# Transposing loads in the head, row-group score matmuls and a fifth Toeplitz buffer in a gated attention and state-space kernel

## The chip, the core and the metric

The kernel runs on one core of a Trainium2 chip, in bf16 with float32 sums. The metric is the device time of one execution in microseconds (us). TensorE does matmuls and their weight loads, ScalarE activations, VectorE and GpSimd elementwise work; SP, ScalarE and GpSimd issue DMAs, which 16 DMA engines carry out.

## The reference

Two branches of 2048 tokens and 448 channels are mixed by a gate for each token:

```
g = sigmoid(sum(x * gate_w))                       # one number a token
q = x @ wq  (16 heads of 28);  k = x @ wk;  v = x @ wv      # one K and V for all heads
a = softmax(q k^T / sqrt(28)) v @ wo               # all 2048 x 2048 scores, for 16 heads
K[d,l] = Re sum_n C[d,n] exp(dt[d] A[d,n] l) dt[d] B[d,n]   # n = 256, l = 0..2047
y = causal convolution of x with K along the tokens + Dskip * x
out = g * a + (1 - g) * y
```

A, B and C are complex, given as real and imaginary parts of shape 448 x 256; dt is exp(log_dt). The input of the convolution is x as well; B_u is not used.

## The kernel before, in words

**Attention.** Q, K and V are projected from x transposed (channels on partitions). The Q rows are laid out in groups of 32 partitions, one head each (28 rows and one row for a bound that is subtracted ahead of the exponential). There are 1024 score tiles of 128 keys x 512 queries: 16 steps (4 groups of heads x 4 quarters of the queries) of 64 tiles. They are put into sets of alternately three and two tiles, 410 in all. For each set TensorE computes the scores into five PSUM banks (`qk`, L1117), ScalarE takes one exponential over the whole set into a ring of 15 tiles (L1153), and TensorE multiplies four tiles with V (`pv`, L1157 and L1163). A score matmul is made in one of two ways: by row groups (L1125), where the matmuls of a set take 29 rows each in different row groups of the array, or at full height (L1133), with a copy of Q in which the rows of all other heads are zero (`qM`). The first six sets and, from the fourteenth on, the sets of three use row groups; the others use full height. `qM` is filled for every step by four small DMAs from GpSimd's queue, in `qproj` (L764).

**Convolution.** `prep_params` (L686) makes seeds from A, B, C and dt; `masters` and `tables` on VectorE build powers of the exponentials for 32 channels at a time; `kgen` (L898) multiplies them into K on TensorE; K goes through a DRAM scratch, and `tload` (L946) brings it back as Toeplitz matrices of 128 x 1024 for four channels at a time (T buffers, four of them, and later three in the space that the used-up U leaves). `conv` (L959) multiplies them with U, which holds x by token blocks.

**Head.** x is loaded in four quarters, transposed on TensorE against an identity (L597), copied from PSUM by ScalarE (L607) and VectorE (L609), and projected. The largest absolute key (`kap`, L640) gives the bound row `Wb` that the second part of the Q projection (L783) needs, so the first scores wait for all of K. The six parameter arrays are loaded and transposed in the same way (L713). U is made from staged rows of x with copies on GpSimd (L550) and a DMA of U onto U.

**The order of the work.** Each engine runs a fixed list, written by a planner in the program (`schedule`, L158) from assumed durations and priorities: lower priority numbers go first among what can start at the same time. Its constants include `SLACK`, by which work of priority 2 and more is put off. Every edit to an operation or an assumed duration can therefore change the order on every engine. DMAs of one queue start in that order; each T, K and U load is issued by SP, the K stores and small attention DMAs by GpSimd.

The functions that the change touches, and what calls them, with the line numbers of the profile:

Of the kernel before, what the change touches and what calls it, by code (L numbers as in the profile page):

```python
# [19 lines left out]
DT = 112  # L20
# [11 lines left out]
NTR = 4  # L32
# [3 lines left out]
XQ = NT * 512  # L36
SIN2PI = 6.2831850
# [37 lines left out]
class Prog:  # L75
# [11 lines left out]
    SLACK = {"pe": 500.0, "dve": 1000.0}  # L87
# [45 lines left out]
    def dma(self, pairs, desc, slot, rd=(), wr=(), pr=0, eng="sp", slow=False, extra=0):  # L133
        kw = dict(allow_slow_non_contiguous=True) if slow else {}

        def fn(e):
            return [e.dma_start(o, i, **kw) for o, i in pairs]  # L137
        nd, size = desc
        ns = 10.0 if size < 64 else 13.0 + 0.033 * size if size < 1500 else 8.0 + 0.0372 * size
        o = self.op(eng, fn, nd * ns / 16.0 * (1.15 if size < 1500 else 1.8 if nd < 512 else 1.0), rd, wr, pr)  # L140
# [233 lines left out]
def el(n, rate=0.96, fix=68):  # L374
    return fix + n / rate
# [15 lines left out]
class Kernel:  # L391
# [25 lines left out]
    def alloc(self):  # L417
# [7 lines left out]
        self.qM = sb("qM", 2 * 4 * 512, BF)  # L425
# [35 lines left out]
        self.XS = nc.dram_tensor("XS_scratch", (3 * DT * XQ,), BF).ap()  # L461
        self.R = nc.dram_tensor("R_scratch", (16 * 4 * 512,), F32).ap()

    def consts(self):
# [5 lines left out]
        dm(V(self.cst, 512, 256), 0.0, 170, [("cst", 1)])  # L470
        pm(V(self.ident, 0, P), 1.0, 200, ["id"])
# [13 lines left out]
        for k in range(2):  # L485
            pm(V(self.qM, k * XQ, XQ), 0.0, 1800, [("qM", k)], 1.5)
        pm(V(self.identf, 0, P), 1.0, 200, ["msq"], 2)
        pg.op("pool", lambda e: e.affine_select(
            out=V(self.identf, 0, P), in_=V(self.identf, 0, P), compare_op=ALU.is_equal, fill=0.0,
            base=0, pattern=[[-1, P]], channel_multiplier=1), 300, rd=["msq"], wr=["msq"], pr=2)  # L490
        self.sel = self.onT.cast(F32)
# [8 lines left out]
    def loads(self):  # L500
        pg, ins = self.pg, self.ins
        self.xst = self.tab
        x = ins["A_x"]

        def lx(q):
            pg.dma([(self.xst.v(0, P, q * 4 * D, [[1, 4 * D]]), dram(x, q * 4 * P * D, [[4 * D, P], [1, 4 * D]]))],
                   (128, 3584), f"x{q}", wr=[("xst", q)])
# [5 lines left out]
        def lraw(k):  # L513
            pg.dma([(raw.v(0, DT, k * 1024, [[1, 1024]]), dram(ins[names[k]], 0, [[1024, DT], [1, 1024]]))],
                   (112, 2048), f"raw{k}", wr=[("raw", k)])
# [4 lines left out]
        pg.dma([(wks.v(0, DT, 0, [[1, 112]]), dram(ins["A_wk"], 0, [[112, DT], [1, 112]])),  # L520
                (wks.v(0, DT, 112, [[1, 112]]), dram(ins["A_wv"], 0, [[112, DT], [1, 112]])),
# [62 lines left out]

    def prep_x(self):
        pg = self.pg
        xst, kT = self.xst, self.kT
        sm = self.small
        for q in range(4):
            for hp in range(2):  # L590
# [657 lines left out]
```

## Time and profile before

| | us |
|---|---|
| median of 3 runs | 521.37 (519.04 to 526.63) |
| the profiled execution | 521.35 |
| its span | 519.4 |
| ScalarE busy | 483.6 (93%) |
| VectorE busy | 447.5 (86%) |
| TensorE busy | 431.1 (83%) |
| GpSimd busy | 161.6 (31%) |
| first exponential starts | 27.69 |
| last exponential ends | 504.17 |
| mean granted TensorE clock | 0.95 |

A group of instructions is shown as line, engine, operation, tiles, shape and count, then the busy time, the mean duration of one in ns, and the idle time just before them with what ended it. The mean durations of overlapping instructions add up to more than the busy time: an exponential over three tiles takes 1561 ns and one over two 1139, but one starts before the other is done, and 410 of them keep ScalarE busy for 465.8 us. The granted clock is 1.00 at full speed.

### The profile page before, as it was taken

The numbers are of one execution on the slowest core, as the hardware profiler recorded it, in microseconds if no ns is written. First come the engines' busy times: TensorE is split into PE (matmuls) and PEld (weight loads), VectorE is DVE, ScalarE is ACT, GpSimd is POOL, SyncE is SP. The second block draws the span as 40 slices with busy tenths as digits, with TensorE's granted clock in tenths as the row PEclk, the third lists the DMA queues.
The fourth block names the chain that finished last, engine by engine and source line by source line (L and its number), as shares of the span: only waits on it lengthen the run. The fifth ranks groups of instructions, "written<-read, shape, count | busy, mean of one in ns | idle before, by whom it ended". The sixth has DMA issues, their size and how long they took to land.

```text
span 519.4 us, 18307 instructions
## 1 busy us (share of the span) xinstructions
PE 431.1 (83%) x8123; PEld 192.9 (37%) x8234; DVE 447.5 (86%) x798; ACT 483.6 (93%) x431; POOL 161.6 (31%) x299
## 2 busy tenths in 40 slices
PE   5778967888878789988878889988888889798884
PEld 4522111324334334434333434433344344443342
DVE  3877899999999999999999979999999989952123
ACT  3699899999999999999999999999999999899980
POOL 5014321612413442424214242432414233315100
PEclk9858587979999999999999999999999999999998
DMA  8995395497991998899998899899996999999996
GB/s 263 259 236 157 28 79 139 120 364 251 288 365 54 321 350 256 271 342 347 316 367 296 279 373 276 285 336 350 329 330 212 304 370 353 346 282 305 376 365 172
DMA packets 121997, 144.31 MB, mean 278 GB/s; under 512 B 53860, under 2 KB 60564, under 8 KB 121920
## 3 DMA queue, kind: packets, MB, share of 16 engines
q1 hardware_dynamic: 112368, 133.06, 81.3%
q0 software_dynamic: 8896, 9.53, 6.8%
q8 instruction: 64, 1.05, 0.8%
q10 hardware_dynamic: 656, 0.57, 0.4%
q14 instruction: 13, 0.11, 0.1%
HBM read 128.76 MB, written 5.23 MB: 258 GB/s over the span
## 4 chain that ended last, share of the span: by engine, by line
ACT 40%; DVE 36%; PE 17%; DMA 3%; issue 2%; ACTq 0%; SPq 0%
ACT expT L1153 40%; DVE tab L868 6%; PE psS L1133 4%; DVE tab L880 3%; DVE tab L879 3%; DVE tab L878 3%; PE psB L1163 3%; PE psS L1125 3%; DVE tab L890 3%; DVE tab L877 3%; DMA T<-KP_scratch 2%; DVE tmp L886 2%; DVE msq L811 1%; DVE cst L984 1%; PE psX L915 1%
## 5 line engine op out<-in xcount | busy, mean ns | idle before, releaser
L1153 ACT ACTIVATE expT<-psS 128x1536 bf16<-128x1536 f32 (+1 forms) x410 | 465.8, 1349 | 8.1 <-PE psS L1125 5.3
L1133 PE MATMUL psS<-qM,kT 128*128 128x512 bf16 x308 | 106.6, 402 | 35.5 <-ACT expT L1153 21.7
L1125 PE MATMUL psS<-qT,kT 29*128 29x512 bf16 x609 | 84.0, 401 | 27.8 <-ACT expT L1153 23.4
L1163 PE MATMUL psB<-expT,vaug 128*32 128x512 bf16 x1024 | 105.4, 403 | 1.1 <-ACT expT L1153 0.6
L137 POOL DMA_DIRECT2D KP_scratch<-kstg x112 | 62.3, 563 | 121.3 <-DVE kstg L930 114.6
L868 DVE TENSOR_TENSOR tab<-tab,mbf 128x512 bf16<-128x512 bf16 (+3 forms) x56 | 64.5, 1152 | 0.0
L1163 PEld LDWEIGHTS psB<-expT,vaug 128*32 128x32 bf16 x1024 | 26.2, 93 | 83.2 <-issue 78.7
L137 POOL DMA_DIRECT2D qM<-qT x64 | 32.0, 507 | 67.9 <-DVE qT L786 42.9
L1125 PEld LDWEIGHTS psS<-qT,kT 29*128 29x128 bf16 x609 | 20.1, 91 | 72.6 <-ACT expT L1153 60.2
L1133 PEld LDWEIGHTS psS<-qM,kT 128*128 128x128 bf16 x415 | 26.0, 98 | 54.8 <-ACT expT L1153 40.2
L137 POOL DMA_DIRECT2D rdenB<-R_scratch x60 | 30.5, 514 | 38.5 <-DMA R_scratch<-denT 27.9
L880 DVE TENSOR_TENSOR tab<-tab 128x128 bf16<-128x128 bf16 (+4 forms) x70 | 41.8, 597 | 0.0
L879 DVE TENSOR_TENSOR tab<-tab 128x128 bf16<-128x128 bf16 (+4 forms) x70 | 41.8, 597 | 0.0
L974 PE MATMUL psS<-T,U 128*32 128x128 bf16 (+7 forms) x1600 | 39.0, 220 | 2.2 <-DMA T<-KP_scratch 1.3
L974 PEld LDWEIGHTS psS<-T,U 128*32 128x32 bf16 (+7 forms) x1600 | 27.1, 94 | 18.1 <-issue 12.2
L137 POOL DMA_DIRECT2D denT<-acc x15 | 10.9, 726 | 69.1 <-DVE acc L1030 45.0
L890 DVE TENSOR_TENSOR tab<-tab,tmp 128x4096 bf16<-128x4096 bf16 x14 | 32.1, 2290 | 0.1
L878 DVE TENSOR_TENSOR tab<-tab,mbf 128x4096 bf16<-128x4096 bf16 x14 | 31.9, 2280 | 0.1
L877 DVE TENSOR_TENSOR tab<-tab,mbf 128x4096 bf16<-128x4096 bf16 x14 | 32.0, 2283 | 0.0
L974 PE MATMUL psX<-T,U 128*32 128x128 bf16 (+7 forms) x1216 | 29.9, 223 | 1.0 <-issue 0.9
L974 PEld LDWEIGHTS psX<-T,U 128*32 128x32 bf16 (+7 forms) x1216 | 21.0, 95 | 14.7 <-issue 11.3
L915 PE MATMUL psX<-tab 128*32 128x64 bf16 x1024 | 24.8, 241 | 1.1 <-DVE qT L786 0.4
(153 smaller groups left out, 517.1 us busy)
## 6 DMA issues: line engine op xcount, KB each, us to landing
T<-KP_scratch SPq DMA_DIRECT2D x176, 512.0 KB, 8.7
U<-KP_scratch SPq DMA_DIRECT2D x48, 512.0 KB, 9.6
rdenB<-R_scratch POOLq DMA_DIRECT2D x60, 64.0 KB, 5.7
U<-cst SPq DMA_DIRECT2D x1, 3584.0 KB, 18.7
qM<-qT POOLq DMA_DIRECT2D x64, 32.0 KB, 5.1
tab<-in_A_x_dram SPq DMA_DIRECT2D x4, 448.0 KB, 6.2
O<-in_A_x_dram SPq DMA_DIRECT2D x16, 112.0 KB, 2.7
O<-cst SPq DMA_DIRECT2D x1, 1792.0 KB, 28.6
```

Source lines behind the costliest of these rows:

```text
L137: return [e.dma_start(o, i, **kw) for o, i in pairs]
L868: vo(lambda e, dst=dst, src=src, mri=mri: e.tensor_tensor(dst, src, mri, ALU.mult), 4 * n, done + mk(lv), [kr, ki, tk])
L877: vo(lambda e, src=src, mi=mi, tv=tv: e.tensor_tensor(tv, src, mi, ALU.mult), 2 * n, done + mk(lv), [tk])
L878: vo(lambda e, dst=dst, src=src, mr=mr: e.tensor_tensor(dst, src, mr, ALU.mult), 2 * n, done + mk(lv), [kr, ki, ("gap", s)])
L879: vo(lambda e, dc=dc, tc=tc: e.tensor_tensor(dc[0], dc[0], tc[1], ALU.subtract), n, [tk, kr], [kr])
L880: vo(lambda e, dc=dc, tc=tc: e.tensor_tensor(dc[1], dc[1], tc[0], ALU.add), n, [tk, ki], [ki])
L890: vo(lambda e: e.tensor_tensor(tab.v(0, P, FM, [[4, 1024], [1, 4]]), tab.v(0, P, lo + 124, [[CG, 32], [-4, 32], [1, 4]]), rho.v(0, P, 0, [ ...
L974: r = e.matmul(ps.v(32 * j, 32 - 2 * n, 128 * k, [[1, 128]]), self.U.v(0, P, (4 * gi + j) * 32 + 2 * n, [[1, 32 - 2 * n]]), tbuf.v(0, P, t ...
L1125: r = e.matmul(self.psS.v(0, P, 512 * b, [[1, 512]]), kT.v(32 * h, DH + 1, 128 * kt, [[1, 128]]), qT.v(32 * h, DH + 1, 512 * (i % 2), [[1, ...
L1133: return e.matmul(self.psS.v(0, P, 512 * b, [[1, 512]]), kT.v(0, P, 128 * kt, [[1, 128]]), self.qM.v(0, P, (i % 2) * XQ + 512 * h, [[1, 51 ...
L1153: pg.op("act", lambda e: e.activation(expT.v(0, P, 512 * es[0], spread(es, n)), self.psS.v(0, P, 512 * bs[0], spread(bs, n)), AF.Exp, scal ...
L1163: r = e.matmul(self.psB.v(32 * h, 32, 0, [[1, 512]]), vaug.v(0, P, 32 * kt, [[1, 32]]), expT.v(0, P, 512 * ring[t], [[1, 512]]), start=(kt ...
```

## The change

- x is loaded by transposing DMAs straight into its transposed place, in quarters of 512 tokens, with channels in three blocks of 128 and one of 64 instead of four of 112 (`KT`). The last 16 tokens of the last block come by a small DMA of single elements. The transposes on TensorE and the copies from PSUM are gone, and the weights of the projections are loaded in the same blocks.
- The six parameter arrays are loaded by transposing DMAs; the products on VectorE read SBUF instead of PSUM. Products of priority 3 are placed behind the maximum of the keys.
- U is loaded straight from x, in rows of 256 B (128 B in the last region); its layout is now region, token block, channel, so the stationary operand of the convolution has a step of 128 channels between its columns. The staging, GpSimd's copies and the DMA of U onto U are gone.
- All score sets use row groups; `qM`, its memsets and its DMAs are gone.
- There are five T buffers from the start (`NTR`).
- `kgen` writes both halves of K into one PSUM bank and stores them with one addition and one copy instead of two each; the four T loads of a convolution stand together ahead of its matmuls.
- The planner's `SLACK` for VectorE goes from 1000 to 700 ns, and a float32 identity for the gate moves into another buffer.

```diff
-NTR = 4
+NTR = 5
+KT = (128, 128, 128, 64)
-    SLACK = {"pe": 500.0, "dve": 1000.0}
+    SLACK = {"pe": 500.0, "dve": 700.0}
...
+            if flip:
+                return [e.dma_start_transpose(o, i) for o, i in pairs]
...
-        self.qM = sb("qM", 2 * 4 * 512, BF)
...
         def lx(q):
-            pg.dma([(self.xst.v(0, P, q * 4 * D, [[1, 4 * D]]), dram(x, q * 4 * P * D, [[4 * D, P], [1, 4 * D]]))],
-                   (128, 3584), f"x{q}", wr=[("xst", q)])
+            xT, xo = self.xq(q)
+            at = lambda off, n, m: xT.v(0, P, xo + off, [[512, n], [1, m]])
+            r = q * 512 * D
+            if q < 3:
+                pg.dma([(at(0, 4, 512), dram(x, r, [[D, 512], [1, 512]]))], (512, 1024), f"x{q}", wr=self.xk(q), flip=True, cost=1900)
+                return
+            pg.dma([(at(0, 3, 512), dram(x, r, [[D, 512], [1, 384]])),
+                    (at(1536, 1, 496), dram(x, r + 384, [[D, 496], [1, 128]]))],
+                   (512, 896), f"x{q}", wr=[("xT", q)], flip=True, cost=1900)
...
         def lraw(k):
-            pg.dma([(raw.v(0, DT, k * 1024, [[1, 1024]]), dram(ins[names[k]], 0, [[1024, DT], [1, 1024]]))],
-                   (112, 2048), f"raw{k}", wr=[("raw", k)])
+            pg.dma([(raw.v(0, P, k * 1024, [[D, 2], [1, D]]), dram(ins[names[k]], 0, [[NM, D], [1, NM]]))],
+                   (448, 512), f"raw{k}", wr=[("raw", k)], flip=True, cost=900)
...
+        xT, xo = self.xq(3)
+        pg.dma([(xT.v(0, 64, xo + 2032, [[1, 16]]), dram(x, 2032 * D + 384, [[1, 64], [D, 16]]))],
+               (1024, 2), "x4", wr=[("xT", 4)], eng="act", slow=True)
...
+        part = lambda r, odd, off, dims: bass.AP(tensor=self.U.h, offset=odd * rs + r * TW + off, ap=[[2 * rs, 64]] + dims)
+        for r in range(4):
+            w = min(128, D - 128 * r)
+            self.late.append(pg.dma(
+                [(part(r, 0, 16 * w, [[256, w // 16], [1, 256]]), self.cst.v(0, 64, 512, [[0, w // 16], [1, 256]])),
+                 (part(r, 0, 0, [[w, 16], [1, w]]), dram(x, 128 * r + 960 * D, [[D, 64], [-64 * D, 16], [1, w]])),
+                 (part(r, 1, 0, [[w, 32], [1, w]]), dram(x, 128 * r + 1984 * D, [[D, 64], [-64 * D, 32], [1, w]]))],
+                (3584, 2 * w), f"u{r}", rd=[("cst", 1)], wr=[("U", r)], pr=0.3).i)
...
         def trans(k, pr):
-            t_ = self.grp()
...
-            pg.op("pe", mm, 700, rd=[("raw", k), "id"], wr=[X, "rawdone"], pr=pr, lock=t_)
-            return t_, X
+            return raw.v(0, P, k * 1024, [[D, 2], [1, D]]), ("raw", k)
...
-            pg.dma([(self.qM.v(32 * h, 32, s * XQ + 512 * h, [[1, 512]]), self.qT.v(32 * h, 32, 512 * s, [[1, 512]]))
-                    for h in range(4)], (128, 1024), f"qm{s}", rd=[("q", s)], wr=[("qM", s)], pr=0, eng="pool", extra=4500)
...
+        pg.op("dve", lambda e: e.tensor_copy(ko.v(0, P, 0, [[64, 8], [1, 63]]), G.v(0, P, 0, [[64, 8], [1, 63]])),
+              el(504), rd=[X], wr=["kst"], pr=2, unlock=G)
...
-                                     self.U.v(0, P, (4 * gi + j) * 32 + 2 * n, [[1, 32 - 2 * n]]),
+                                     self.U.v(0, P, uo + 2 * n * uw + j, [[uw, 32 - 2 * n]]),
...
-            if s < 6 or s >= 14 and len(ts) == 3:
-                rd = set()
...
-            else:
-                for t, b in zip(ts, bs):
...
+            pg.op("pe", row, 220, rd=sorted(rd, key=str), wr=bk, pr=0, mode="q", ni=2 * len(ts))
```

## The prediction

> **What bounds the kernel now.** I read the page from the top, then busy time by stage, the stretches in which the clock was low, the waits, and the timeline at both ends of ScalarE's work. The columns of a stretch are: window, its length, busy us and instructions of TensorE, weight loads, VectorE, ScalarE and GpSimd, then the granted clock, the DMA engines' share and GB/s.
>
> ```profile
> PE 431.1 (83%) x8123; PEld 192.9 (37%) x8234; DVE 447.5 (86%) x798; ACT 483.6 (93%) x431; POOL 161.6 (31%) x299
> ...
> L1153 ACT ACTIVATE expT<-psS 128x1536 bf16<-128x1536 f32 (+1 forms) x410 | 465.8, 1349 | 8.1 <-PE psS L1125 5.3
> L1133 PE MATMUL psS<-qM,kT 128*128 128x512 bf16 x308 | 106.6, 402 | 35.5 <-ACT expT L1153 21.7
> L1125 PE MATMUL psS<-qT,kT 29*128 29x512 bf16 x609 | 84.0, 401 | 27.8 <-ACT expT L1153 23.4
> ```
>
> ScalarE is busy for 93%, and 465.8 us of that are the 410 exponentials, which wait only 8.1 us in all. Most waits of the score matmuls are for the exponential.
>
> ```profile
> 27.69:504.17 476.48, 406.39 (x7791) 174.62 (x7900) 424.01 (x752) 468.80 (x414) 153.96 (x277) 0.95 0.90 281
> ...
> 460.00:480.00 20.00, 17.29 (x451) 8.65 (x457) 7.36 (x12) 20.00 (x19) 9.45 (x18) 1.00 0.94 297
> ```
>
> The first exponential starts at 27.69; the last ends at 504.17. Between them ScalarE is busy 468.80 of 476.48 us, so 7.7 us is lost there. The chain that ended last gives VectorE 36%, but from 460 VectorE is busy 7.36 of 20 us while ScalarE still has 44 us to go: two saturated engines run side by side, and ScalarE is the one that ends late. The span is thus 27.7 (before the first exponential) + 476.5 + 15.2 (after the last) = 519.4; the profiled execution took 521.35, so 1.95 lies around the span, and the median of the runs (521.37) is the same. Three terms can move: the head, the 7.7 us of holes, the tail. The exponentials themselves don't change.
>
> ```profile
> 50.59:64.25 13.66, 12.94 (x53) 2.40 (x55) 11.77 (x28) 11.76 (x11) 6.13 (x6) 0.50 0.33 24
> 84.73:91.55 6.82, 5.92 (x81) 1.80 (x81) 6.82 (x15) 6.53 (x6) 0.00 (x0) 0.50 0.09 16
> 105.21:112.03 6.82, 6.15 (x59) 1.67 (x56) 6.82 (x9) 5.89 (x6) 0.56 (x1) 0.50 1.06 395
> ...
> 120.00:440.00 320.00, 278.57 (x5866) 126.68 (x5937) 312.35 (x558) 318.20 (x282) 108.53 (x200) 1.00 0.93 305
> ```
>
> Of the 7.7 us, 1.90 + 0.29 + 0.93 = 3.1 are in these three stretches at a clock of 0.50, 0.9 more before 42 us, also cold, and 1.8 in the 320 us from 120 on, where the clock was 1.00 (the rest, some 1.9, is at 92 and around 450). So a cold TensorE costs ScalarE about 1 us per stretch of 7 to 14 us, and a warm one almost nothing.
>
> **The change, part by part.**
>
> *Head.* Today x goes through 64 transposes on TensorE (7.4 us busy), four copies of 1.02 us on ScalarE and four of 1.21 on VectorE; two of the parameters go through TensorE too before the first exponential. All of that is removed, and the DMA engines transpose. The new chain: the last x quarter lands, its keys are projected, ScalarE copies them, VectorE takes their maximum, and the second half of the Q projection follows. In the changed order VectorE is given the product with A_re ahead of the last maximum and the product with B_re ahead of the last Q copy, so both must have landed as well. On the SP queue they stand behind all of x: three quarters of 512x512 and one of 520 KB are 2.09 MB, and the three parameters up to B_re 0.69 MB; ScalarE's queue adds W_q and log_dt, 0.52 MB. No transposing DMA is in the trace. Its nearest rows by size are these: copies in pieces of 448 B moved at 30 ns a piece on each of 16 engines, which is 237 GB/s. The end below is a plain load: the 3,584 B pieces of x were all started by 10.5 us, though seven loads shared the engines. The end above is the copy U<-U in pieces of 32 B: 0.92 MB between 58.35 and 76.56 us, 50 GB/s.
>
> At 237 GB/s, 3.30 MB take 13.9 us; with the issue at 0.81 and some 2.5 until data flow (the first load had landed at 4.29), the last x quarter is there at about 15, A_re at 16.2, B_re at 17.2. TensorE has had little to do by then, so I take the cold row for its key projection (1.89; warm it took 1.03): 15.2 + 1.9 = 17.1, key copy 0.69, maximum 0.68 (18.5), the last maximum and Wb 0.4 (18.9, with its semaphore 19.0), then in order on VectorE the B_re product 1.08, the V copy 0.58 and the Q copy 0.69 (21.4), then the scores, 0.63. First exponential at **22.0** instead of 27.69: **-5.7**. With a plain load's landing the same chain gives 17 to 18 (-10), with the 32 B rate 2.78 MB last 56 us and the first exponential comes at some 63 (+35); I take the middle row because its pieces are nearest in size to the rows that are transposed. The head breaks even when B_re lands 5.7 us later, at 23, which is about 165 GB/s.
>
> [...]
>
> *Score matmuls.* 410 weight loads and as many matmuls with the zero-padded Q (full height) become row-group matmuls of 29 rows, which run beside each other: a set of two cost 0.60 us full and 0.39 by row groups when warm, 1.03 and 0.60 when cold. 205 sets x 0.21 = 43 us less work for TensorE. None of it lies on the path while ScalarE is busy, so I count it at nothing; it is worth something only in the holes. The 64 Q copies on GpSimd's queue (0.50 us each, 32 us) and two 1.8 us memsets go as well; GpSimd is busy 31%, its other DMAs mostly wait for VectorE, and nothing ended later because of it.
>
> *The clock* is what that could cost. From 36.9 to 40.4 us every set used the padded form, and at 40.35 the clock rose to 1.00; in the mixed stretches it fell again at 50.59, 71.07, 84.73 and 105.21 whenever no table or convolution matmuls ran, and from 112 on, where they did, it stayed at 1.00 for 402 us. With fewer cells at work I expect TensorE cold through the first phase, until the convolutions come (the changed order has them 40 score tiles, some 18 us, earlier), and a few cold stretches later. When cold, row groups need 1.03 - 0.60 = 0.4 us less a pair, which takes the holes of 38.55 and 41.15 away (0.9); the first Q projection into a cold array stays (1.9), the first convolution too (0.9). I take three more cold stretches than before at about 0.9 us each: -0.9 + 2.7 = **+1.8**.
>
> *Fifth buffer and smaller things.* One hole, 0.80 us at 266, was a wait for a Toeplitz buffer's load, which five buffers should hide; the last convolution's pieces, now out of the end, cost 0.68 + 0.42 = 1.1 there, since the changed order has no convolution left after the last exponential: **-1.9**. Storing K as one eviction instead of two saves VectorE about 28 x 0.41 - 14 x 0.68 = 2.0 us and 2.4 of the small additions; VectorE isn't what ends, so nothing. The first half of K now waits for the second (64 matmuls, at 40 in 0.81 some 1.3 us) before GpSimd stores it, beside a landing of 8.7 us for the load behind it. On SP the eleven transposing issues, at 0.43 as plain ones, are hidden by their own data; x reloads and the scratch copies of x become two issues each, off the path. U is loaded in rows of 256 B instead of through staging, eight GpSimd copies of 1.03 and a 20 us copy; the first convolution needs it only at some 90 us. The stationary reads of the convolution now step 256 B from column to column where they were contiguous. The trace has loads in steps of 8 B (the K matmuls) but none like it; between no cost and a doubling of its 68.9 us (39.0 and 29.9 in its two largest groups) I take none, as the 8 B rows show none. The doubling would fit in 120 to 440, where TensorE is idle 41 of 320 us and gets 30 back from the scores, but narrowly.
>
> *Sum.* -5.7 + 1.8 - 1.9 = -5.8: 521.35 - 5.8 = **515.5 us**.
>
> **The rivals.**
>
> *A: the clock holds.* If what counts is whether TensorE is at work at all, row groups do as well as full height and the cleared head is pure gain: no added cold stretches (-2.7), the remaining cold holes of 3.1 halve (-1.5), x lands nearer to the plain rate (-2.5): 508.8 us. For it: from 170 to 177 two stretches with little convolution passed at 1.00. Against it: 12.94 busy of 13.66 us from 50.59 on, at 0.50. [...]
>
> *B: the clock doesn't hold, and ScalarE starves* (slower). Place: 120 to 440. There a pair of sets takes ScalarE 2.30 us (6.89 for six exponentials), and one of 28 convolutions comes every 14 us or so. Cold, 6.3 pairs at 0.61 + 0.60 + 0.78 are 12.5 us of TensorE and the 128 matmuls of a convolution, at 1.07 per 32, are 4.3: more than 14. So each cold stretch costs the 0.93 us of the one at 111, or more. From 8 added stretches on it has eaten the other gains (7.6). At half the time cold, 400 us hold some 29 stretches of 6.8: 521.35 - 7.6 + 27 = 541 us.
>
> *C: transposing DMAs are slow.* At 110 GB/s 3.3 MB last 30 us, first exponential at 38: +10, less 0.1: 531.7 us. Against it speaks only the distance to the 32 B row.
>
> *D: the change is nothing*, because the head is bound elsewhere (table loads and the Sin and Exp on ScalarE, 5 us in a row): 521 us. The changed order does remove the transposes, so only the head's gain is in doubt.
>
> **How the numbers follow.** Chances: forecast (511 to 520) 0.42, A 0.27, B 0.14, C 0.09, D 0.08. A measurement of this kernel can tell about 2% (10.4 us) from no change: under 510.9 is faster, over 531.8 slower. Most of A and a little of the forecast are under: 0.27. Most of B and half of C are over: 0.18. The rest, 0.55, is within. The range leaves out the best of A and the worst of B and C: 504 to 534.
>
> **What would show it.** First exponential near 22 us, and x landed by 15 to 16; the clock's row at 5 for most of the slices from 20 to 80 us and mostly 9 after 110; exponentials' idle time near 9 us; no convolution after the last exponential and some 14 us from there to the end. I am wrong if the head doesn't move, if ScalarE's idle time goes over 15 us with a clock under 0.9 after 120, or if the weight loads of the convolution have grown.

## The result and the profile after

The changed kernel takes 590.36 us (median of 4 runs, 588.73 to 592.09), against 521.88 us for the kernel before on the same chip: a ratio of 1.130, 95% interval 1.121 to 1.139. It is **slower by 13%**, where the prediction said 515.5 us and gave 504 to 534 as the range. The profiled execution took 588.73 us, its span 586.8. Executions more than 1.5% slower than the fastest of their kernel are left out of all ratios and intervals below, but not out of the medians.

The first fence is from the page of the changed kernel: busy time of the engines, the granted clock in 40 slices, then groups of instructions (busy time, mean ns of one, idle time just before them and what ended it).

```profile
PE 489.5 (83%) x8105; PEld 232.5 (40%) x8122; DVE 489.0 (83%) x766; ACT 532.4 (91%) x427; POOL 126.4 (22%) x231
...
PEclk9999995785797999998668759966799999897977
...
L1132 ACT ACTIVATE expT<-psS 128x1536 bf16<-128x1536 f32 (+1 forms) x410 | 518.3, 1463 | 18.5 <-PE psS L1115 17.6
L1115 PE MATMUL psS<-qT,kT 29*128 29x512 bf16 x1024 | 190.8, 462 | 64.5 <-ACT expT L1132 60.8
...
L964 PEld LDWEIGHTS psX<-T,U 128*32 128x32 bf16 (+6 forms) x1472 | 46.8, 190 | 13.6 <-issue 12.5
...
L964 PEld LDWEIGHTS psS<-T,U 128*24 128x24 bf16 (+7 forms) x1440 | 44.8, 194 | 11.7 <-issue 10.2
...
L863 DVE TENSOR_TENSOR tab<-tab,mbf 128x4096 bf16<-128x4096 bf16 x14 | 39.3, 2807 | 0.0
```

Four things differ from before, and two of them the prediction had not in its sum. The same 410 exponentials keep ScalarE busy for 518.3 us instead of 465.8: "the exponentials themselves don't change" is what the prediction took for granted. The convolution's weight loads take 190 to 194 ns each where they took 94 to 95. VectorE's product over 4096 columns, which the change doesn't touch, takes 2807 ns instead of 2283. And the clock's row, which was 9 from the tenth slice on, now goes down to 5 to 8 again and again to the end, while the exponentials wait 18.5 us instead of 8.1. These are the lines of before for the last three:

```profile
PEclk9858587979999999999999999999999999999998
...
L974 PEld LDWEIGHTS psS<-T,U 128*32 128x32 bf16 (+7 forms) x1600 | 27.1, 94 | 18.1 <-issue 12.2
...
L877 DVE TENSOR_TENSOR tab<-tab,mbf 128x4096 bf16<-128x4096 bf16 x14 | 32.0, 2283 | 0.0
...
L974 PEld LDWEIGHTS psX<-T,U 128*32 128x32 bf16 (+7 forms) x1216 | 21.0, 95 | 14.7 <-issue 11.3
```

The 9s at the start of the changed kernel's row mislead. Its record of the clock begins only with the first change, at 83.22 us, and the row shows 9 where there is no record. The matmuls over 512 columns take 582 to 634 ns up to 80 us and 384 to 391 from 85 to 90, so the clock was at one half from the start to 83 us; in the kernel before it first rose at 13.05. The same goes for the rows of the changed kernel with the old U and with rows of U 272 B apart, below (first change at 90.47 and 84.30).

The next answer has the whole stretch of the exponentials and, for comparison with the 320 us that the prediction showed at a clock of 1.00, three stretches from its middle. Columns: window, its length, busy us and instructions of TensorE, weight loads, VectorE, ScalarE and GpSimd, granted clock, DMA share, GB/s.

```profile
33.19:571.10 537.91, 464.55 (x7977) 221.50 (x7992) 469.29 (x724) 520.61 (x413) 122.07 (x208) 0.85 0.76 247
```

```profile
300.00:320.00 20.00, 17.97 (x361) 9.15 (x360) 18.73 (x33) 17.52 (x14) 2.33 (x4) 0.70 0.90 316
320.00:340.00 20.00, 16.81 (x264) 8.12 (x269) 17.02 (x16) 18.05 (x14) 5.87 (x11) 0.72 1.02 323
340.00:360.00 20.00, 19.25 (x303) 8.16 (x300) 18.12 (x38) 16.95 (x14) 5.73 (x10) 0.68 0.39 126
```

So the span is now 33.19 before the first exponential (27.69 before the change), 537.91 from there to the end of the last (476.48), and 15.7 after it (15.2). The 67.4 us that the span grew are +5.5, +61.4 and +0.5. Of the 61.4 us in the middle ScalarE's busy time accounts for 520.61 - 468.80 = 51.8, and idle time for the other 9.6: from 300 to 360 ScalarE stands still for 7.5 of 60 us, at a clock of about 0.7. Of the 17.3 us that ScalarE is idle between the first and the last exponential, 14.1 lie in the 207 us at the half clock (the start up to 83.22 counted in) and 3.2 in the 331 us at the full clock.

What makes the same exponentials longer can be counted in the trace: for each exponential, how many weight loads of the convolution started while it ran, and the mean duration by that number (in ns, from the first to the last record of each instruction; an exponential begins before the one ahead of it has ended).

| | before, two tiles | before, three tiles | after, two tiles | after, three tiles |
|---|---|---|---|---|
| no weight load | 1123 | 1539 | 1105 | 1531 |
| 8 to 15 | 1162 | 1568 | 1231 | 1779 |
| 24 to 39 | 1168 | 1605 | 1557 | 2112 |
| 40 and more | 1236 | 1572 | 1895 | 2522 |

Most rows are means of 9 to 132 instructions; the last one of before, two tiles, is a mean of two. Without weight loads beside them the exponentials are what they were; beside the new loads they take up to 1.7 times as long. The product over 4096 columns behaves alike: 2283 ns where no such load runs beside it, 3167 beside 12 or more; before the change it was 2286 and 2281. That product reads and writes SBUF alone; an exponential reads PSUM and writes SBUF, and which of its two accesses is held up isn't shown.

### The profile page after: what moved, and what is told of

Same layout as the page of the kernel before. It is cut to its first block, busy times and chain, and to the rows that moved or that the text cites. A ratio compares the mean times of both kernels' runs of the same rounds, so it can differ in the third digit from the quotient of the medians.

```text
span 586.8 us, 18050 instructions
## 1 busy us (share of the span) xinstructions
PE 489.5 (83%) x8105; PEld 232.5 (40%) x8122; DVE 489.0 (83%) x766; ACT 532.4 (91%) x427; POOL 126.4 (22%) x231
## 4 chain that ended last, share of the span: by engine, by line
ACT 38%; DVE 32%; PE 26%; DMA 2%; issue 1%; SPq 0%; ACTq 0%
ACT expT L1132 38%; PE psS L1115 9%; PE psB L1142 5%; DVE tab L854 4%; DVE tab L866 3%; DVE tab L876 3%; DVE tab L864 3%; DVE tab L865 3%; DVE tab L863 2%; DMA T<-in_A_x_dram 2%; PE psS L964 2%; PE psX L964 2%; DVE tmp L872 1%; PE psS L901 1%; DVE acc L1020 1%; DVE cst L974 1%
## 5 line engine op out<-in xcount | busy, mean ns | idle before, releaser
L1132 ACT ACTIVATE expT<-psS 128x1536 bf16<-128x1536 f32 (+1 forms) x410 | 518.3, 1463 | 18.5 <-PE psS L1115 17.6
L1115 PE MATMUL psS<-qT,kT 29*128 29x512 bf16 x1024 | 190.8, 462 | 64.5 <-ACT expT L1132 60.8
L1142 PE MATMUL psB<-expT,vaug 128*32 128x512 bf16 x1024 | 122.2, 467 | 0.9 <-ACT expT L1132 0.5
L1115 PEld LDWEIGHTS psS<-qT,kT 29*128 29x128 bf16 x1024 | 40.4, 94 | 154.3 <-ACT expT L1132 133.0
L964 PE MATMUL psX<-T,U 128*32 128x128 bf16 (+6 forms) x1472 | 55.4, 275 | 0.2 <-DVE qT L776 0.2
L964 PEld LDWEIGHTS psX<-T,U 128*32 128x32 bf16 (+6 forms) x1472 | 46.8, 190 | 13.6 <-issue 12.5
L964 PEld LDWEIGHTS psS<-T,U 128*24 128x24 bf16 (+7 forms) x1440 | 44.8, 194 | 11.7 <-issue 10.2
L139 POOL DMA_DIRECT2D R_scratch<-denT x15 | 10.5, 702 | 136.5 <-DVE denT L1026 67.4
L863 DVE TENSOR_TENSOR tab<-tab,mbf 128x4096 bf16<-128x4096 bf16 x14 | 39.3, 2807 | 0.0
L872 DVE TENSOR_TENSOR tmp<-tmp,mq 128x64 bf16<-128x64 bf16 (+4 forms) x70 | 27.1, 387 | 0.1
L797 DVE TENSOR_TENSOR msq<-seedz 128x512 f32<-128x512 f32 (+1 forms) x40 | 26.6, 664 | 0.1
L901 PE MATMUL psS<-tab 128*32 128x64 bf16 x896 | 20.7, 244 | 0.6 <-DVE tab L881 0.4
```

The source lines that it names most:

```text
L863: vo(lambda e, src=src, mi=mi, tv=tv: e.tensor_tensor(tv, src, mi, ALU.mult), 2 * n, done + mk(lv), [tk])
L872: vo(lambda e, w=w, lv=lv: e.tensor_tensor(rho.v(0, P, 2 * w, [[64, 32], [2, w], [1, 2]]), rho.v(0, P, 0, [[64, 32], [2, w], [1, 2]]), sel ...
L964: r = e.matmul(ps.v(32 * j, 32 - 2 * n, 128 * k, [[1, 128]]), self.U.v(0, P, uo + 2 * n * uw + j, [[uw, 32 - 2 * n]]), tbuf.v(0, P, to + j ...
L1115: r = e.matmul(self.psS.v(0, P, 512 * b, [[1, 512]]), kT.v(32 * h, DH + 1, 128 * kt, [[1, 128]]), qT.v(32 * h, DH + 1, 512 * (i % 2), [[1, ...
L1132: pg.op("act", lambda e: e.activation(expT.v(0, P, 512 * es[0], spread(es, n)), self.psS.v(0, P, 512 * bs[0], spread(bs, n)), AF.Exp, scal ...
L1142: r = e.matmul(self.psB.v(32 * h, 32, 0, [[1, 512]]), vaug.v(0, P, 32 * kt, [[1, 32]]), expT.v(0, P, 512 * ring[t], [[1, 512]]), start=(kt ...
```

## The experiments

The theory after this comparison (W in the expectations): the stationary reads of U, which now step 256 B from column to column, take twice as long and slow ScalarE's and VectorE's accesses to SBUF while they run. The rivals: the clock that row groups leave (K, later C), and the transposing loads with the fifth buffer and the head (L).

### The old U in the changed kernel, and the new step in the kernel before

```diff
 # the changed kernel with U staged, copied and read as before
-  self.U.v(0, P, uo + 2 * n * uw + j, [[uw, 32 - 2 * n]])
+  self.U.v(0, P, (4 * gi + j) * 32 + 2 * n, [[1, 32 - 2 * n]])
```

> The changed kernel with U loaded and laid out as before (32 columns of one channel side by side, so that the convolution's weight loads step 2 B from column to column); heads, row groups and the fifth buffer stay. Theory W (weight loads that step 256 B take twice as long and slow ScalarE's and VectorE's accesses to SBUF meanwhile): the exponentials' busy time falls from 518.3 back to 465 to 470 us, weight loads of the convolution from 190-194 to about 95 ns, span 522 to 535. Rival K (row groups hold the clock down and that stretches and starves everything): weight loads get shorter, the exponentials stay above 505 us busy, span 575 to 587. Rival L (the transposing loads and the head): also above 575.

```diff
 # the kernel before with the address of the stationary read alone
-  self.U.v(0, P, (4 * gi + j) * 32 + 2 * n, [[1, 32 - 2 * n]])
+  self.U.v(0, P, uo + 2 * n * uw + j, [[uw, 32 - 2 * n]])   # uw = 128, 64 in the last block
```

> The kernel before with one thing changed: the convolution's stationary reads step 256 B (128 B for the last four channel groups) from column to column, through the same block of U, so that it multiplies other elements of U than the reference asks for; every other instruction is the same. Theory W: exponentials from 466 to 510-520 us busy, weight loads about 190 ns, span 519 + 50 to 65 = 570 to 585. Rivals K and L: 519 to 524, exponentials 466.

The old U in the changed kernel: 541.09 us (ratio to before 1.036, interval 1.027 to 1.044), so 49.3 of the 68.5 us go with it; its span of 536.8 is just above the 522 to 535 that W expected. The new step alone in the kernel before: 576.38 us (1.104, 1.097 to 1.111), +54.8, with 570 to 585 expected. These are the page's lines of the kernel before with the new step, clock first:

```profile
PEclk9858768699999999999999999999999999999998
...
L1155 ACT ACTIVATE expT<-psS 128x1536 bf16<-128x1536 f32 (+1 forms) x410 | 523.3, 1463 | 6.0 <-PE psS L1127 2.8
...
L976 PEld LDWEIGHTS psS<-T,U 128*18 128x18 bf16 (+7 forms) x1600 | 49.2, 199 | 13.3 <-issue 11.1
```

And these are the same lines of the changed kernel with the old U:

```profile
PEclk9999999559997899969779899988688997997877
...
L1137 ACT ACTIVATE expT<-psS 128x1536 bf16<-128x1536 f32 (+1 forms) x410 | 467.6, 1318 | 20.3 <-PE psS L1120 19.7
...
L969 PEld LDWEIGHTS psS<-T,U 128*32 128x32 bf16 (+7 forms) x1536 | 27.3, 99 | 13.9 <-issue 10.0
```

The two effects come apart cleanly. The step puts 57.5 us on the exponentials (523.3 - 465.8) with the clock at 9 from the ninth slice on and even less idle time than before (6.0). Taking the step away gives the 50.7 us back (518.3 - 467.6), and leaves the low clock and 20.3 us of idle time. W is right for some 50 us, which no rival explains; but 19.6 us of the loss (541.09 - 521.54) are something else.

### From which step on

The kernel before, in which only the step of the stationary reads is changed again. The first run went with the two above, the other four later.

```diff
-  uw = 128, 64 in the last block
+  uw = 8 | 16 | 32 | 64   # in all blocks
+  uw = 120, 60 in the last block
```

> As the kernel before with the convolution's stationary reads stepping 16 B (other elements of U than the reference asks for). Theory W does not say from which step the cost begins. If each 2 B read that falls into a new 16 B piece of a row pays in full: as with 256 B, 570 to 585. If the cost comes from far steps or from a power of two: 519 to 530.

> The kernel before with the convolution's stationary reads stepping 32 B (other elements of U than the reference asks for). 16 B gave 126 ns a weight load (95 before), exponentials 466.9 us busy and 522.9; 256 B gave 199 ns, 523.3 us and 576.4. If the price is paid for each column that lies in a new 16 B piece, and no more for farther ones: as 16 B, 120 to 140 ns, exponentials 466 to 470, 520 to 526. If it grows with the step: 140 to 160 ns, exponentials 470 to 485, 525 to 540.

> The same with 64 B. By the first reading as 16 B (520 to 526); by the second 160 to 180 ns, exponentials 480 to 500, 535 to 555. If 64 B is a boundary from which a read costs a line of its own: already as 256 B, 570 to 580.

> The same with 128 B. If the price grows with the step: 180 to 200 ns, exponentials 500 to 515, 550 to 570; if it begins only at 256 B: 520 to 530.

> The same with 240 B (120 B in the last four groups), which is no power of two. If the columns collide because a step of 256 B always comes to the same part of the memory: exponentials below 490 us busy, 525 to 545. If distance alone counts: as 256 B, 199 ns, exponentials 515 to 525, 570 to 580.

| step | weight load, ns | exponentials busy, us | time, us | ratio to before (95%) |
|---|---|---|---|---|
| 2 B (before) | 94 to 95 | 465.8 | 521.54 | |
| 16 B | 126 to 127 | 466.9 | 522.89 | 1.001 (0.998 to 1.004) |
| 32 B | 129 | 466.1 | 523.60 | 1.002 (0.998 to 1.006) |
| 64 B | 130 to 131 | 466.2 | 523.73 | 1.003 (0.999 to 1.007) |
| 128 B | 162 to 163 | 468.0 | 524.98 | 1.005 (1.001 to 1.009) |
| 240 B | 128 | 466.6 | 524.58 | 1.004 (1.001 to 1.008) |
| 256 B | 199 | 523.3 | 576.38 | 1.104 (1.097 to 1.111) |

This was not foreseen by theory W, which had spoken of wide steps. A step of 240 B costs no more than one of 16 B, and 256 B costs 52 us more than 240. (The rows of 240 and 256 B are means with the last block, which has half the step.) The row for 240 B on its page:

```profile
L1155 ACT ACTIVATE expT<-psS 128x1536 bf16<-128x1536 f32 (+1 forms) x410 | 466.6, 1328 | 8.4 <-PE psS L1127 5.7
...
L976 PEld LDWEIGHTS psS<-T,U 128*32 128x32 bf16 (+7 forms) x1600 | 32.0, 128 | 18.2 <-issue 12.1
```

Two prices have to be kept apart. The first begins with 16 B or below: loads take 126 to 131 ns with steps of 16, 32, 64 and 240 B, a third more than the 94 to 95 with 2 B (at 128 B 162 to 163, 70% more), and the exponentials stay within 2.2 us of before. Between 2 and 16 B no load of U was tried; the loads of `kgen`, which step 8 B, take 116 to 117 ns for 32 columns in the kernel before, where those of U take 97 with 2 B and 138 with 16 B. Whether that price goes by pieces of 16 B, as two of the expectations have it, isn't shown. The price that made this kernel slow isn't that one: it comes with 256 B, doubles the load (199 ns), and is paid by the other engines.

### The changed kernel with rows of U 272 B apart

If it is the one number 256, the changed kernel needs no other layout, only a gap.

```diff
 TW = 4 * 1024
+UP = 136
+UB = 32 * UP
...
-  uw = min(128, D - 4 * gi // 128 * 128)
-  uo = 4 * gi // 128 * TW + 4 * gi % 128
+  uw = UP if gi < 96 else 64
+  uo = 4 * gi // 128 * UB + 4 * gi % 128
 # the loads of U and the T buffers in its space follow the new rows
```

> The changed kernel with one size changed: the rows of U lie 272 B apart instead of 256 B in the first three blocks (128 B in the last, as in the changed kernel); T's unused tail of 768 columns is given up for the room. Theory P (columns a power of two apart, 256 B, collide; 240 B did not): weight loads 125 to 135 ns, exponentials 466 to 471 us busy, 535 to 546, as with the old U (541.1). If it is distance (a step of 256 B or more): unchanged, 585 to 592.

```profile
PEclk9999998569597999988878899978779689997876
...
L1135 ACT ACTIVATE expT<-psS 128x1536 bf16<-128x1536 f32 (+1 forms) x410 | 469.0, 1298 | 23.6 <-PE psS L1118 22.7
...
L967 PEld LDWEIGHTS psS<-T,U 128*32 128x32 bf16 (+7 forms) x1440 | 31.1, 132 | 12.3 <-issue 10.3
```

Eight unused columns between the rows bring the exponentials from 518.3 back to 469.0 us and the loads from 194 to 132 ns, both as expected; a step longer than 256 B does no more harm than one of 16 B, so it is not distance. The time, 553.12 us (1.052, 1.042 to 1.062; 546.38 to 561.20), is above the 535 to 546 that were expected: the exponentials wait 23.6 us, with a low clock (of ScalarE's 22.4 idle us between the first and the last, 18.3 lie at the half clock). That part is the next question.

### Row groups alone

```diff
 # the kernel before
-  if s < 6 or s >= 14 and len(ts) == 3: row groups, else full height
+  row groups in all sets; qM, its memsets and its DMAs removed
 # first run with NTR = 5, second with NTR = 4
```

> The kernel before with all score sets by row groups, no padded copies of Q and five Toeplitz buffers; head and U as before. Theory W: exponentials 465 to 470 us busy, span 514 to 525 (what my prediction gave to these two parts, 0 and -1.9, and the clock +1.8). Rival K: exponentials above 500 us busy or idle above 20 us, span 560 to 590.

> The kernel before with all score sets by row groups and no padded copies of Q, four Toeplitz buffers. The earlier run with five gave 541.2, exponentials idle 28.3 us, 153.6 us at the half clock between 60 and 540. Theory C (the sets by row groups leave TensorE less to do, the clock falls again and again, scores come late): 535 to 548, over 100 us at the half clock between 60 and 540. Rival T (the fifth buffer, its earlier transfers and other places of the convolution in the order make the loss): 519 to 526, clock as before (23.9 us at half).

With five buffers 541.21 us (1.034, 1.025 to 1.043), with four 532.22 (1.013, 1.007 to 1.020). So row groups lose 9 us with the padded copies and their DMAs gone and nothing else edited; that is under 2%, but its interval leaves out zero. The first run's time fits neither W nor K, and the second is 3 us below the 535 that C gave. In the trace of the second the granted clock falls 14 times between 60 and 540 us, for 120 us, against 4 falls with 24 us in the kernel before (added up from the record of the clock in each trace). Here, in the table below and in the expectations only falls that begin in that window are counted; with those that began earlier it is 151 against 28 us. The exponentials wait 18.6 us instead of 8.1 and are busy for 2.9 us more. Between the first and the last exponential ScalarE is idle for 16.0 of 176 us at the half clock and for 2.4 of 314 at the full clock; in the kernel before it is 3.8 of 43 and 3.9 of 433. So the added wait is all at the half clock, and theory C, which is rival B of the prediction, holds in its mechanism.

The changes of the clock lie whole numbers of 3.41 us apart in these traces (in the kernel before at 13.05, 23.29, 40.35, 50.59, 64.25 and 71.07, for one), so what TensorE did ahead of a change is read here in stretches of that length. First the kernel before: two stretches with little on TensorE, each with the one behind it. Columns: window, its length, busy us and instructions of TensorE, granted clock, DMA share, GB/s.

```profile
262.22:265.63 3.41, 2.18 (x60) 1.00 1.06 317
265.63:269.04 3.41, 2.86 (x72) 1.00 1.05 382
405.58:408.99 3.41, 2.18 (x30) 1.00 0.99 328
408.99:412.40 3.41, 2.96 (x79) 1.00 1.05 320
```

Then the kernel with row groups and four buffers:

```profile
295.61:299.02 3.41, 2.45 (x34) 1.00 0.96 291
299.02:302.43 3.41, 3.41 (x79) 0.50 1.04 353
370.70:374.11 3.41, 2.50 (x34) 1.00 1.07 357
374.11:377.52 3.41, 3.36 (x59) 0.50 1.05 381
```

With full-height sets in the mix, TensorE was busy for only 2.18 of 3.41 us and the clock stayed; with row groups it fell after 2.45 and 2.50. After 60 us the kernel before has 4 falls, none behind a stretch with more than 2.12 us of busy time. Busy time alone doesn't decide, but the falls go with little of it: after 60 us no fall in any of the traces begins behind a stretch with more than 2.85 us.

### More busy time, and other doses of full height

In the sets that had full height before, each row-group matmul is issued twice with the same operands and output:

```diff
-  for t, b in zip(ts, bs):
+  for t, b in list(zip(ts, bs)) * dup:      # dup = 2 where the set was at full height, else 1
```

> As the kernel before with row groups and four buffers, but in every set that had full-height matmuls before, each row-group matmul is issued twice with the same operands and the same output, so that TensorE is busy about as long as with full height while the same few rows of the array work. Theory C, read as busy time of TensorE: the clock holds (under 50 us at half between 60 and 540), 519 to 527. Theory C2 (the clock goes by how much of the array works): falls stay, 535 to 550. Rival R (a row-group set comes late for a reason other than the clock): the loss stays at a clock that holds.

> The changed kernel with U as before (541.1 in the earlier run) and the doubled row-group matmuls in the sets that had full height. Theory C by busy time: the clock holds, 541 - 15 to 20 = 520 to 527, with the head's loss still in it. C2 or R: 535 to 548.

On the kernel before it gives 558.87 us (1.067, 1.061 to 1.073), on the changed kernel with the old U 557.40 (1.064, 1.057 to 1.071). The first two lines below are from the page of the former, the third is an answer on its start.

```profile
PE 502.4 (91%) x8649; PEld 202.3 (37%) x8649; DVE 444.7 (80%) x798; ACT 489.6 (88%) x431; POOL 124.4 (22%) x233
...
PEclk9855555758779687999989899997999899999658
```

```profile
30.00:98.20 68.20, 64.68 (x451) 0.50 0.54 101
```

TensorE is busy for 64.68 of 68.20 us and the clock stays at one half all that time; in falls that begin between 60 and 540 us it is low for 102 us (120 without the doubling), and with the long one that began before 60 for 141 (151). So busy time alone does not hold the clock. The times are above what any theory gave (550 and 548 at most) and say less than was hoped: the doubled work also pushes other work back. In the second of the two runs the exponentials wait only 16.7 us, but 32.8 us pass after the last of them, in which TensorE still has convolutions to do.

The opposite doses: in the kernel before, every second set of two by row groups as well, and all sets from the seventh on at full height.

```diff
-  if s < 6 or s >= 14 and len(ts) == 3:
+  if s < 6 or s >= 14 and s % 4 != 3:       # half
+  if s < 6:                                  # full
```

> The kernel before with every second two-tile set also by row groups: about 210 score matmuls at full height instead of 415 (none in the run with row groups alone: 532.2, 120 us at the half clock between 60 and 540; before: 24 us). If the clock follows how much of the array works (theory C2), the loss goes with the dose: 40 to 100 us at the half clock, 524 to 530. If only the kind of the last sets matters, no change: 520 to 524.

> The kernel before with all sets but the first six at full height (1009 matmuls instead of 415). Theory C2: no falls after 112 us, and fewer before it; TensorE has more to do, so 519 to 527. If full height were only a cost of TensorE time, which is off the path: same as before with the same falls.

| score matmuls at full height | us at half clock, falls that begin in 60 to 540 | exponentials wait, us | time, us | ratio to before (95%) |
|---|---|---|---|---|
| 0 (four buffers) | 120 | 18.6 | 532.22 | 1.013 (1.007 to 1.020) |
| 218 | 57 | 9.9 | 524.18 | 1.003 (0.999 to 1.008) |
| 415 (before) | 24 | 8.1 | 521.57 | |
| 1009 | 0 | 39.5 | 571.95 | 1.095 (1.089 to 1.101) |

```profile
PE 516.1 (91%) x8234; PEld 215.1 (38%) x8234; DVE 447.2 (79%) x798; ACT 502.2 (88%) x431; POOL 161.0 (28%) x299
...
PEclk9859999999999999999999999999999999999997
```

The time at the half clock goes with the dose, down to nothing (the page of the last row is shown); TensorE is as busy here (91%) as with the doubled row groups, and the clock's row is the opposite. What differs is how many rows of the array a score matmul uses, 128 or 29. That the clock goes by just that isn't shown, and one fall speaks against it: with the new head alone (below) the clock falls at 27.91 us behind a stretch in which TensorE was busy for all 3.42 us, mostly with V projections of 128 and 64 rows but only 29 columns. Shown is that the time at the half clock follows the number of full-height matmuls, and that busy time doesn't explain it. The last row missed its expected 519 to 527 by far: at full height all through, TensorE is busy for 516.1 us and the exponentials wait for it; of ScalarE's 39.1 idle us between the first and the last, 38.5 lie at the full clock. The kernel before sits between the two losses.

### The head, and the buffer on the new head

The changed kernel's head with U, score sets and buffers as before, then the same with another order on TensorE, then the changed kernel with the old U and four buffers:

```diff
 # head alone: the changed kernel with NTR = 4, qM, both kinds of score matmuls, U as before
 # another order: V projections of quarters 1 to 3 behind the scores of the second set,
 # first Q projection behind the last key projection
-  pg.op("pe", mv, 900, ..., pr=0.5)
+  pg.op("pe", mv, 900, ..., pr=1.3)
+  pg.after[first matmul of qproj(0)] = self.k3
+  pg.after[k] = scores of set 1, for k in self.mv[1:]
 # old U, four buffers
-NTR = 5
+NTR = 4
```

> The changed kernel's head alone (x, parameters and weights by transposing transfers), with U, score sets and four buffers as before. My prediction gave the head -5.7; the trace of the changed kernel has its first exponential at 33.19 us against 27.69, so +5.5 if nothing is given back: 525 to 529. If the later first exponential is given back because the convolution starts no later: 519 to 523.

> The head alone (529.7) with another order on TensorE: the last key projection ahead of the first Q projection, and the V projections of the last three quarters behind the scores of the first two sets. If the head's loss is TensorE's order at the half clock: first exponential at 27 to 29 us instead of 32.83, time 523 to 527. If the loss is elsewhere (V projections only come to stand in the way later, or the transfers): 528 to 532.

> The changed kernel with U as before and four Toeplitz buffers instead of five: it differs from the run with the head alone (529.7) by the row groups only, and from 541.1 by the buffer only. If the row groups cost what they did on the kernel before (532.2 against 523.3): 536 to 542, and the buffer is worth nothing. If the fifth buffer costs, as 541.2 against 532.2 on the kernel before suggests: 529 to 534.

The head alone takes 529.70 us (1.011, 1.007 to 1.016): a loss of 6.4 us, and not a gain of 5.7. The first exponential starts at 32.83, 5.1 us later than before. The changes to `kgen`, to the order of the T loads and to `SLACK` are in this run too, so how much of the 6.4 us is the head's alone isn't separated. This is TensorE's start in the changed kernel (start, us, line, tiles, shape, count, and the idle time before with what ended it):

```profile
17.11 2.00 PE L612 MATMUL psS<-expT 128*128 128x512 bf16 x4 [0.67 <-DMA expT<-in_A_x_dram]
20.98 2.00 PE L764 MATMUL psX<-xT,Wq 128*128 128x512 bf16 x4 [1.88 <-DVE Wq L554]
22.91 2.00 PE L612 MATMUL psS<-expT 128*128 128x512 bf16 x4
24.85 1.40 PE L628 MATMUL psB<-expT,xT 128*128 128x29 bf16 x16
26.18 1.40 PE L628 MATMUL psB<-expT,T 128*128 128x29 bf16 x16
27.51 2.73 PE L628 MATMUL psB<-expT 128*128 128x29 bf16 x32
30.58 2.02 PE L764 MATMUL psS<-xT,Wq 128*128 128x512 bf16 x4 [0.33 <-issue]
32.53 1.03 PE L1115 MATMUL psS<-qT,kT 29*128 29x512 bf16 x5
```

The last key projection stands behind the first Q projection, which waits until 20.98 for VectorE's copy of W_q; then 64 V projections take 5.4 us at the half clock (24.85 to 30.24) ahead of the second part of the Q projection and the scores. Before, the clock rose at 13.05, amid the transposes that the change removes, and 16 V projections took 0.55 to 0.63 us instead of 1.40; whether the missing transposes keep the clock low in the new head wasn't tested. In the other order the last key projection runs when its quarter has landed, and the scores at 27.55:

```profile
19.18 2.00 PE L622 MATMUL psS<-expT 128*128 128x512 bf16 x4 [0.32 <-DMA expT<-in_A_x_dram]
21.11 2.00 PE L775 MATMUL psX<-xT,Wq 128*128 128x512 bf16 x4
...
27.55 1.03 PE L1129 MATMUL psS<-qT,kT 29*128 29x512 bf16 x5
```

The first exponential starts at 28.21 instead of 32.83, and the time is 526.09 us (1.008, 1.004 to 1.011). So TensorE's order was most of the delay of the first exponential, 4.6 of 5.1 us. Of the time it gives back less: 3.6 us between the two medians, which come from different chips, and some 2 by the two ratios. The transfers had their part too: the last quarter of x is there at 19.2 in this run and at 19.7 in the changed kernel, not at 15. Its two transposing transfers were issued only at 14.70 and 16.12 there, because the issues ahead of them on SP took 1.4 to 5.4 us each, and from 5 to 10 us the DMA engines moved 127 GB/s, from 10 to 15 us 161. None of the versions tried is faster than the kernel before. This one, the best with the new head, is above it by some 4 us, of which the later first exponential is 0.5; the exponentials wait 11.7 us instead of 8.1.

The fifth buffer: 544.62 us with four (1.044, 1.038 to 1.049) against 541.09 with five on the new head, but 532.22 against 541.21 on the old one. The sign differs, and single runs of these kernels lie 2 to 8 us apart, with mean clocks that differ as well (with five on the new head, 537.43 us at 0.898 and 544.24 at 0.818). A gain or loss by the buffer itself can't be read from this, and 544.62 is above both expectations. Row groups cost 14.9 us on the new head (544.62 - 529.70, two chips; some 17 by the ratios) and 9 on the old.

## Why the prediction was wrong, step by step

**The stationary reads of U: this step failed, and it is 50 us.** The prediction had the operation before it ("step 256 B from column to column where they were contiguous"), bounded it between nothing and a doubling of the convolution's 68.9 us, and took nothing because it saw no cost in the loads in steps of 8 B. These take 116 to 117 ns for 32 columns, against 97 for the contiguous ones of U: no sign of the large price, but not nothing. For TensorE the upper end was generous: the loads doubled, from 48.1 us of busy time in the two groups (27.1 + 21.0) to 91.6 (46.8 + 44.8), but with the step alone the matmuls went from 68.9 only to 97.5. But the sum looked at TensorE only. That time would have fitted beside the exponentials, as was argued (with the step alone they wait 6.0 us, and 8.1 before); what was left out is that ScalarE and VectorE are slower while these reads run (exponentials over three tiles 2522 ns instead of 1531, the product over 4096 columns 3167 instead of 2283), so that a cost off the path lands on the engine that sets the end. The price for it: 54.8 us alone, 49.3 in the changed kernel. The row that was taken as the nearest, 8 B, was near in kind and far in size; nothing between 8 and 256 B was in the trace, and even 240 B would have confirmed the wrong price.

**"The exponentials themselves don't change"** fell with it: 465.8 to 518.3 us busy.

**The clock (+1.8) and the score matmuls (0): wrong in size.** The direction was right and so was the mechanism: with row groups the clock falls more often, and ScalarE waits. Three added falls of 0.9 us were taken; there were ten (14 against 4 after 60 us) in the row-group kernel with four buffers, and the cost was 9 us there, 14.9 on the new head. The prediction's sign, cold from 20 to 80 us, came too, though the clock's row shows 9 there; but it had the clock mostly full after 110, and from 120 to the last exponential it was 0.85. Rival B, with 0.14, described this part: it gave 541 us, and the changed kernel without the step of U takes 541.09, though with 14 falls instead of B's 29, and without the gains that B deducted, so that the two numbers meet is in part luck. Rival A, that work alone holds the clock, is refuted by 64.68 busy of 68.20 us at 0.50.

**The head (-5.7): wrong sign.** Measured +6.4, with the smaller changes in it. Two terms of its chain failed. The last quarter of x was put at 15 and came at 19.7: the 237 GB/s of plain copies was too high for this mix of transposing and plain loads (127 GB/s from 5 to 10 us, 161 from 10 to 15, 225 from 15 to 20), rival C's 110 GB/s (first exponential at 38) was too low, and the transposing issues on SP, taken at 0.43 us each and as hidden, took 1.3 to 5.4. But B_re was there at 22.2, just ahead of the 23 at which the prediction had the head break even. The rest fits the second term: the chain counted VectorE's order and not TensorE's. There 64 V projections, 5.4 us at the half clock, stand ahead of the second part of the Q projection, and the key projection behind a wait for W_q. It had taken the half clock for the key projection, and for no V projection. The other order took 4.6 us off the first exponential.

**Fifth buffer and tail (-1.9): not confirmed.** No convolution is left after the last exponential, as predicted, but the time from there to the end is 15.7, not 14. For the buffer no sign can be given. Row groups (9 to 14.9 us) and the head (6.4) together make 15 to 21 of the 19.6 us that are left without the step of U, so no large part is missing.

**What was right:** that ScalarE's exponentials set the end; that the sum has to go by the head, the holes and the tail; and that longer weight loads would be the sign of a wrong price. Of the three signs that were named for being wrong, two came (the head doesn't move forward, longer weight loads of the convolution) and one nearly: ScalarE was idle for 17.3 us between the first and the last exponential, 13.9 of them after 120, at a clock of 0.85. The prediction's range had no case with longer weight loads in it, though it named the sign: a doubling that "fits narrowly" should have been a rival with a price of its own.

## What to carry to other kernels

When a change alters the layout of an operand, price its new access step for every engine that uses SBUF at the same time, not only for the engine that reads it, and avoid a step of exactly 256 B in stationary reads: a gap of 16 B between the rows took the exponentials from 518.3 back to 469.0 us here. Before you take work away from TensorE because it isn't the bound, look whether that work is what holds its clock: from 415 matmuls at full height to none the time at the half clock went from 24 to 120 us in the falls counted, and ScalarE paid for it. And follow a new head through the order on every engine, at the half clock, which lasted to 83.22 us here; where the clock's row shows 9 at the start, look at the durations of the matmuls (582 to 634 ns over 512 columns, against 384 to 391 after the rise).

## What the runs showed of the hardware

- Weight loads of bf16 columns: 94 to 95 ns with a step of 2 B in the kernel before, 126 to 131 with 16, 32, 64 and 240 B, 162 to 163 with 128 B, 199 with 256 B, 132 to 136 with 272 B. At 256 B they grow with the number of columns from 18 (157 ns) to 30 (227), in the kernel before with that step; those of 32 columns, the first of each eight, take 200.
- Only at 256 B do ScalarE and VectorE become slower beside them: exponentials over three tiles from 1531 to 2522 ns beside 40 loads and more, VectorE's 4096 columns from 2283 to 3167. Why this step and not 240 or 272 B wasn't shown; that the step is a power of two fits, and 128 B, with the loads half-way, fits as well, though there the exponentials take no longer beside loads than without (1524 and 1487 ns). 512 B wasn't tried.
- The clock stayed at one half for 68 us with TensorE busy for 95% of the time, where all score matmuls used 29 of the array's rows, fell once behind 3.42 us without a pause, mostly V projections of 128 and 64 rows and 29 columns, and stayed at full for 522 us in a kernel with 1009 matmuls of 128 rows; in the kernel before, with 415 of them, it stayed through stretches with TensorE busy for 2.18 of 3.41 us.
- Transposing loads took SP 1.3 to 5.4 us each to issue in the changed kernel's head and landed 3.4 to 12.1 us after their issue began; plain loads of x in the kernel before took 0.38 to 0.43 us to issue.
